# Mean and variance sums by a column of ones, 1/std spread by VectorE transposes, state read in a layer-1 bank

## The chip, the cores and the metric

The kernel runs on one core of one Trainium2 chip. The metric is the time of one execution in microseconds (us); the median of three timed runs is compared. Engines are named TensorE (PE, with its weight loads as PEld), VectorE (DVE), ScalarE (ACT), GpSimd (POOL) and SyncE (SP).

## What is computed

Three stages run one after the other on 8 batches of 512 tokens and 512 channels (8 heads of 64), with 32 state rows per batch and head.

```
scores = x state^T / 8;  a  = softmax(scores);   xread = a state
scores2 = state x^T / 8; a2 = softmax(scores2);  sread = a2 x
x = concat(xread, sread)                           # (8, 544, 512)
mu, var = mean and variance of x over 512 channels
xn = (x - mu) / sqrt(var + 1e-6) * g_ln
x = x + max(xn w_ch1, 0) w_ch2                     # 512 -> 2048 -> 512
gate = sigmoid(5-tap causal convolution of x);  out = ((x w_val) * gate) w_out
```

The weights come as 64-bit floats and are decoded on the chip.

## The kernel before

Channels lie on partitions and tokens in the free dimension, so a sum over channels is a sum over partitions and over KT = 4 column tiles. Matrix products in the feed-forward run as three fp32r matmuls (`mm3`: high and low halves of both operands). Because xread = a state, the first layer is applied to the attention weights: `m_steps` forms m from the state and w_ch1, and a hidden block f is h = m a (two `mm3`, 6 matmuls of 512 columns). ReLU and the split into halves (`hid`) follow on ScalarE and VectorE, and `second(f)` adds the block to four accumulators (four `mm3`, 12 matmuls). `segment` walks f = 0..15 for a batch and lets `second(f)` run one block late. Division by the standard deviation is put off to the end: after the last block, `second` multiplies the accumulators by a row of 1/std, `rstd_row`, and adds x.

The attention of the next batch, the variance and the state read run as `background` generators, one step per block f. TensorE's order is the program's (`manual_schedule`); the other engines' order comes from a scheduler that weighs priorities and expected times. Batches 0 and 1 are special: they run in halves, interleaved with the decoding of the weights, by `first` and `second`, and take mean and variance in `x1_steps`; batches 2 to 7 use `x1_group`, `x1_mean` and `x1_var`. The 256 state-read tokens of all batches form a ninth batch (`sread_block_steps`, key B).

The parts in question:

- `x1_mean` (and lines 358 to 361 for batches 0 and 1): the mean row over all partitions, 6 fp32r matmuls of 512 columns with the column sums of the state, `sbhl`, against the halves of the attention weights.
- `rstd_of`: the squares, summed over the column tiles, are the stationary operand of four fp32 matmuls with one moving column of ones (L293), then VectorE scales (L296) and GpSimd takes the power -1/2 (L297). Each fp32 matmul is recorded as two.
- `rstd_row`: four fp32 matmuls of 128 columns with the identity (L385) turn 1/std into a row on all partitions, and ScalarE copies it (L390). It runs at the end of each half batch.
- `sread`: 32 groups of small matmuls (L276) into a bank of the pool `at`; VectorE transposes it out (L280).

Three PSUM pools exist: four accumulator banks, two `mm` banks for h, two `at` banks for everything else. Scratch tiles of 128x512 share the tag `t2`, six buffers.

Of the kernel before, what the change touches and what calls it, by code (L numbers as in the profile page):

```python
# [21 lines left out]
P = 128  # L22
# [22 lines left out]
def tile_kernel(ctx: ExitStack, tc: tile.TileContext, xT, xk, stT, sn, w1, w2, wval, wout, convw, gln, ident, out):  # L45
# [9 lines left out]
    def sb(shape, dt, tag, bufs=1):  # L55
        cnt[0] += 1
        return main.tile(shape, dt, tag=tag, bufs=BUFS.get(tag, bufs), name=f"{tag}_{cnt[0]}")
# [31 lines left out]
    nhalf = sb([P, KT], F32, "nhalf")  # L89
    ones = sb([P, 1], F32, "ones")  # L90
    nmean = sb([P, 1], F32, "nmean")
# [176 lines left out]
    def sread(b):  # L268
        a2T = a2s.pop(b)
        xn = loads[b][3]  # L270
        sr = at_ps([P, 2, D])
        for u in range(2):
            for c in range(4):
                for p in range(KT):
                    r = slice(32 * p, 32 * p + 32)
                    nc.tensor.matmul(  # L276
                        sr[r, u, :], lhsT=a2T[u][:, c, r], rhs=xn[:, c, 2 * p + u, :], start=(c == 0), stop=(c == 3)
                    )
        srs = t2([P, 4, 32])
        nc.vector.transpose(srs.rearrange("p t n -> p (t n)"), sr.rearrange("p u d -> p (u d)"))  # L280
        for p in range(KT):
            nc.sync.dma_start(
                out=x1d[b, :, p, :].rearrange("(t j) n -> j t n", j=32), in_=srs[32 * p:32 * p + 32]
            )
# [3 lines left out]
    def rstd_of(key, sqs, n):  # L288
        while len(sqs) > 1:
            nc.gpsimd.tensor_tensor(sqs[0], sqs[0], sqs.pop(), op=ALU.add)  # L290
        var = at_ps([P, n // P])
        for c in range(n // P):
            nc.tensor.matmul(var[:, c:c + 1], lhsT=sqs[0][:, c * P:(c + 1) * P], rhs=ones, start=True, stop=True)  # L293
        rstd = small([P, n // P, 1], F32, "rstd")
        rv = rstd.rearrange("p c o -> p (c o)")
        nc.vector.tensor_scalar(rv, var, 1.0 / DM, 1e-6, op0=ALU.mult, op1=ALU.add)  # L296
        nc.gpsimd.tensor_tensor(rv, rv, nhalf[:, :n // P], op=ALU.pow)  # L297
        rstds[key] = rstd
# [16 lines left out]

    def x1_mean(b):
        sbhl, ahl = coef[b][3], ahls[b]
        mus[b] = mu = at_ps([P, S])
        for u in range(2):
            h, l = sbhl[:, 0, u].to_broadcast([P, P]), sbhl[:, 1, u].to_broadcast([P, P])  # L320
            mm3(mu, h, l, ahl[:, u, 0], ahl[:, u, 1], u == 0, u == 1)
# [3 lines left out]
    def x1_var(b):  # L325
# [9 lines left out]
        nc.gpsimd.tensor_tensor(sqs[0], sqs[0], sqs.pop(), op=ALU.add)  # L335
        yield
# [3 lines left out]
        rstd_of(b, sqs, S)  # L340
        yield

    def x1_steps(b):
# [31 lines left out]
        nc.vector.tensor_tensor(sqs[0], sqs[0], sqs.pop(), op=ALU.add)  # L375
        yield
        yield
        rstd_of(b, sqs, S)
        yield

    def rstd_row(key, n):
        rstd = rstds[key]
        rrow = at_ps([P, n])
        for c in range(n // P):
            nc.tensor.matmul(  # L385
                rrow[:, c * P:(c + 1) * P], lhsT=rstd[:, c].to_broadcast([P, P]), rhs=ident_sb,
                start=True, stop=True,
            )
        r = t2([P, n])
        nc.scalar.copy(r, rrow)  # L390
        return r

    def attention_steps(b):
# [13 lines left out]
        softmax1_out(b)  # L407
        yield
# [9 lines left out]
    def sread_block_steps():  # L418
# [3 lines left out]
        yield  # L422
        mu = at_ps([P, NTS])
        for k in range(KT):
            nc.tensor.matmul(mu, lhsT=nmean.to_broadcast([P, P]), rhs=xs[:, k], start=k == 0, stop=k == KT - 1)
# [17 lines left out]
        rstd_of(B, [sq[0][:, 0], sq[0][:, 1]], NTS)  # L443
# [336 lines left out]
    nc.vector.memset(ones, 1.0)  # L780
    nc.vector.memset(nmean, -1.0 / DM)
# [234 lines left out]
```

## Time and profile before

| | us |
|---|---|
| median of three runs | 925.7 |
| the three runs | 924.37, 926.07, 925.7 |
| the profiled execution: span from first to last instruction | 923.6 |
| TensorE busy in it | 905.1 (98%) |
| VectorE, ScalarE, GpSimd busy | 579.0, 374.7, 179.8 |

The profile is of one execution; its own time is known as its span, 923.6 us, which lies 2.1 us under the median of the runs. A matmul's record is longer than the distance between two starts, because matmuls overlap; what one costs is read from the distance of the starts.

### The profile page before, as it was taken

To read this page: it belongs to the slowest core of one execution; us is meant where nothing else is said; L and a number is where in the kernel's file an instruction comes from. 1 tells how busy PE (TensorE), PEld (TensorE's weight loads), DVE (VectorE), ACT (ScalarE), POOL (GpSimd) and SP (SyncE) were. 2 spreads that over 40 slices of the span, in tenths; PEclk is the share of its full clock that TensorE was granted. 3 is DMA by queue.
4 is the path that set the end of the run, shared out by engine and by line. 5 is a ranking of instruction groups with operands and counts; after the bars stand their busy time and mean duration, and the time that the engine had idled before them with its cause. 6 is when DMAs were issued, how large, how long until landed. Compare 5 with 4: busy or idle time off the path is not lost.

```text
span 923.6 us, 12956 instructions
## 1 busy us (share of the span) xinstructions
PE 905.1 (98%) x5151; PEld 687.6 (74%) x5152; DVE 579.0 (63%) x1004; ACT 374.7 (41%) x688; POOL 179.8 (19%) x155
## 2 busy tenths in 40 slices
PE   7989999999999999999999999999999999999998
PEld 2346766777777677777777777777789988888886
DVE  6997987575358571444427246342449799988871
ACT  4755654243234332332324134231326555555532
POOL 0000000012113421411431141141200022433100
PEclk8999999999999999999999999999999999999999
DMA  9932220012103111110101110110111203222122
GB/s 368 358 117 72 72 73 1 41 54 98 49 1 117 49 49 49 49 49 16 70 15 46 49 46 1 27 46 1 46 69 70 82 18 130 91 92 92 46 91 69
DMA packets 26668, 66.45 MB, mean 72 GB/s; under 512 B 10864, under 2 KB 13040, under 8 KB 22512
## 3 DMA queue, kind: packets, MB, share of 16 engines
q1 hardware_dynamic: 25984, 65.24, 19.8%
q8 instruction: 40, 0.66, 0.3%
q10 hardware_dynamic: 624, 0.40, 0.2%
q14 instruction: 20, 0.16, 0.1%
HBM read 47.80 MB, written 17.83 MB: 71 GB/s over the span
## 4 chain that ended last, share of the span: by engine, by line
PE 89%; DVE 5%; ACT 3%; DMA 2%; issue 1%; SPq 0%; ACTq 0%; DVEq 0%
PE acc L77 16%; PE acc L79 16%; PE acc L78 16%; PE mm L77 9%; PE mm L79 8%; PE mm L78 8%; PE at L138 4%; PE at L77 2%; PE at L78 2%; PE at L79 2%; PE mm L914 1%; PE at L276 1%; PE at L385 1%; DMA big<-in_xT 1%; PE at L262 1%
## 5 line engine op out<-in xcount | busy, mean ns | idle before, releaser
L626 DVE SCALAR_TENSOR_TENSOR hid<-mm,hid 128x512 fp32r<-128x512 f32 (+1 forms) x140 | 92.3, 659 | 210.1 <-ACT hid L624 210.0
L77 PE MATMUL acc<-hid,w 128*128 128x512 f32 (+1 forms) x560 | 213.4, 381 | 2.6 <-DVE x L312 1.8
L79 PE MATMUL acc<-hid,w 128*128 128x512 f32 (+1 forms) x560 | 211.5, 378 | 0.0
L78 PE MATMUL acc<-hid,w 128*128 128x512 f32 (+1 forms) x560 | 211.3, 377 | 0.0
L624 ACT ACTIVATE hid<-mm 128x512 fp32r<-128x512 f32 (+2 forms) x144 | 82.5, 573 | 246.4 <-PE mm L79 243.6
L77 PEld LDWEIGHTS acc<-hid,w 128*128 128x128 f32 x560 | 105.4, 188 | 24.8 <-DVE x L312 2.7
L77 PE MATMUL mm<-ahl,m 128*128 128x512 f32 (+1 forms) x312 | 120.9, 388 | 0.0
L79 PEld LDWEIGHTS acc<-hid,w 128*128 128x128 f32 x560 | 105.4, 188 | 20.0
L78 PEld LDWEIGHTS acc<-hid,w 128*128 128x128 f32 x560 | 105.4, 188 | 19.1
L78 PE MATMUL mm<-ahl,m 128*128 128x512 f32 (+1 forms) x312 | 115.3, 369 | 0.0
L79 PE MATMUL mm<-ahl,m 128*128 128x512 f32 (+1 forms) x312 | 115.2, 369 | 0.0
L74 POOL TENSOR_TENSOR m<-mb,m 128x512 fp32r<-128x512 f32 x48 | 65.4, 1379 | 201.6 <-ACT m L73 201.6
L702 DVE SCALAR_TENSOR_TENSOR ahl<-big,cw,ahl 128x508 f32<-128x508 f32 (+3 forms) x128 | 102.8, 852 | 0.2
L77 PEld LDWEIGHTS mm<-ahl,m 128*128 128x128 f32 x312 | 59.0, 189 | 40.5 <-issue 32.5
L73 ACT ACTIVATE m<-mb 128x512 fp32r<-128x512 f32 x62 | 38.8, 629 | 86.6 <-DVE mb L144 86.5
L79 PEld LDWEIGHTS mm<-ahl,m 128*128 128x128 f32 x312 | 59.0, 189 | 10.1
L78 PEld LDWEIGHTS mm<-ahl,m 128*128 128x128 f32 x312 | 59.1, 189 | 8.5 <-DVE m L74 0.5
L144 DVE SCALAR_TENSOR_TENSOR mb<-cs,sbn,at 128x512 f32<-128x512 f32 x62 | 43.5, 743 | 28.3 <-PE at L138 27.5
L688 POOL TENSOR_TENSOR w<-big,w 128x512 fp32r<-128x512 f32 x24 | 38.2, 1621 | 93.7 <-ACT w L686 93.7
L78 PE MATMUL acc<-w,raw 128*128 128x512 f32 (+1 forms) x144 | 54.3, 377 | 0.0
L79 PE MATMUL acc<-w,raw 128*128 128x512 f32 (+1 forms) x144 | 54.3, 377 | 0.0
L77 PE MATMUL acc<-w,raw 128*128 128x512 f32 (+1 forms) x144 | 54.3, 377 | 0.0
(172 smaller groups left out, 1314.5 us busy)
## 6 DMA issues: line engine op xcount, KB each, us to landing
w<-in_w SPq DMA_DIRECT2D x20, 512.0 KB, 7.1
big<-in_xT SPq DMA_DIRECT2D x8, 1024.0 KB, 4.8
big<-in_xk SPq DMA_DIRECT2D x8, 1024.0 KB, 6.5
x2d<-x SPq DMA_DIRECT2D x8, 1024.0 KB, 3.9
big<-x2d SPq DMA_DIRECT2D x8, 1024.0 KB, 4.8
out<-hid SPq DMA_DIRECT2D x16, 512.0 KB, 2.8
raw<-in_w SPq DMA_DIRECT2D x12, 512.0 KB, 6.4
raw<-in_wval SPq DMA_DIRECT2D x4, 512.0 KB, 3.6
```

Source lines behind the costliest of these rows:

```text
L73: nc.scalar.activation(hi, src, AF.Copy)
L74: eng.tensor_tensor(lo, src, hi.bitcast(F32), op=ALU.subtract)
L77: nc.tensor.matmul(acc, lhsT=wh, rhs=xl, start=first, stop=False)
L78: nc.tensor.matmul(acc, lhsT=wl, rhs=xh, start=False, stop=False)
L79: nc.tensor.matmul(acc, lhsT=wh, rhs=xh, start=False, stop=last)
L138: nc.tensor.matmul(mp[u][32 * p:32 * p + 32, :], lhsT=stg[r, p, :], rhs=w1s[4 * q + p][r], start=True, stop=True)
L144: a = nc.vector.scalar_tensor_tensor(mb, cs[:, q], sbn[:, u], mp[u], op0=ALU.mult, op1=ALU.add)
L262: nc.tensor.transpose(tp[:, c, :], a2[u][:, c * P:(c + 1) * P], ident_sb)
L624: marks["act"] = nc.scalar.activation(hid[:, 0], h, AF.Relu)
L626: marks["dve"] = nc.vector.scalar_tensor_tensor(hid[:, 1], h, 0.0, hid[:, 0].bitcast(F32), op0=ALU.max, op1=ALU.subtract)
L688: nc.gpsimd.tensor_tensor(lo, src, hi.bitcast(F32), op=ALU.subtract)
L702: t = nc.vector.scalar_tensor_tensor(g[:, j:], x[:, :n - j], cw_sb[:, k, PAD - j:TAPS - j], g[:, j:], op0=ALU.mult, op1=ALU.add)
```

## The change

- A helper `halves_of` splits a 128 x n tile into fp32r halves: high on ScalarE, low on GpSimd (or on VectorE where it is scaled). `column_total` multiplies both halves by ones on all 128 x 128 weights: two fp32r matmuls of n columns, the total in every partition.
- Mean of batches 2 to 7: `mean_terms` forms state sum times attention weight for both column tiles (one ScalarE and one VectorE instruction) and splits it one batch ahead; `x1_mean` is a `column_total`. Batches 0 and 1 keep theirs.
- Variance of all batches: the summed squares are split and `column_total` gives the row; VectorE transposes it in blocks of 32, scales, GpSimd takes the power of 16 columns in place of 4.
- `rstd_row` is one VectorE transpose of the broadcast 1/std; its matmuls and its ScalarE copy are gone.
- The state read of batches 2 to 7 goes into an `mm` bank.
- The state tokens' mean: two GpSimd additions, a scaled split and a `column_total` in place of four fp32 matmuls (L425), two steps later.

```
--- before.py
+++ after.py
@@ -86,9 +86,8 @@
     ident_sb = sb([P, P], F32, "ident")
     g_sb = sb([P, KT, 1], F32, "g")
     cw_sb = sb([P, KT, TAPS], F32, "cw")
-    nhalf = sb([P, KT], F32, "nhalf")
-    ones = sb([P, 1], F32, "ones")
-    nmean = sb([P, 1], F32, "nmean")
+    nhalf = sb([P, S // 32], F32, "nhalf")
+    ones = sb([P, 1], F32R, "ones")
     part = sb([P, 1], F32, "part")
     cs = sb([P, NQ, S], F32, "cs")
     halos = []
@@ -268,7 +267,7 @@
     def sread(b):
         a2T = a2s.pop(b)
         xn = loads[b][3]
-        sr = at_ps([P, 2, D])
+        sr = ps(ps_mm, "mm", [P, 2, D]) if b > 1 else at_ps([P, 2, D])
         for u in range(2):
             for c in range(4):
                 for p in range(KT):
@@ -285,16 +284,28 @@
 
     x1s, rstds = {}, {}
 
-    def rstd_of(key, sqs, n):
-        while len(sqs) > 1:
-            nc.gpsimd.tensor_tensor(sqs[0], sqs[0], sqs.pop(), op=ALU.add)
-        var = at_ps([P, n // P])
-        for c in range(n // P):
-            nc.tensor.matmul(var[:, c:c + 1], lhsT=sqs[0][:, c * P:(c + 1) * P], rhs=ones, start=True, stop=True)
-        rstd = small([P, n // P, 1], F32, "rstd")
+    def halves_of(x, n, scale=1.0):
+        hi, lo = (sb([P, n], F32R, "t2") for _ in range(2))
+        nc.scalar.activation(hi, x, AF.Copy, scale=scale)
+        if scale == 1.0:
+            nc.gpsimd.tensor_tensor(lo, x, hi.bitcast(F32), op=ALU.subtract)
+        else:
+            nc.vector.scalar_tensor_tensor(lo, x, scale, hi.bitcast(F32), op0=ALU.mult, op1=ALU.subtract)
+        return hi, lo
+
+    def column_total(out, hl):
+        for i in range(2):
+            nc.tensor.matmul(out, lhsT=ones.to_broadcast([P, P]), rhs=hl[i], start=i == 0, stop=i == 1)
+
+    def rstd_of(key, hl, n):
+        var = at_ps([P, n])
+        column_total(var, hl)
+        turned = t2([P, n // 32, 32])
+        nc.vector.transpose(turned.rearrange("p g n -> p (g n)"), var)
+        rstd = small([P, n // 32, 1], F32, "rstd")
+        nc.vector.tensor_scalar(rstd, turned[:, :, :1], 1.0 / DM, 1e-6, op0=ALU.mult, op1=ALU.add)
         rv = rstd.rearrange("p c o -> p (c o)")
-        nc.vector.tensor_scalar(rv, var, 1.0 / DM, 1e-6, op0=ALU.mult, op1=ALU.add)
-        nc.gpsimd.tensor_tensor(rv, rv, nhalf[:, :n // P], op=ALU.pow)
+        nc.gpsimd.tensor_tensor(rv, rv, nhalf[:, :n // 32], op=ALU.pow)
         rstds[key] = rstd
 
     def x1_group(b):
@@ -313,12 +324,18 @@
             else:
                 nc.scalar.copy(x1[:, k], xp[k])
 
+    def mean_terms(b):
+        sbn, aT = coef[b][2], aTs[b]
+        t = t2([P, S])
+        nc.scalar.activation(t, aT[:, 0], AF.Copy, scale=sbn[:, 0])
+        nc.vector.scalar_tensor_tensor(t, aT[:, 1], sbn[:, 1], t, op0=ALU.mult, op1=ALU.add)
+        terms[b] = halves_of(t, S)
+
+    terms = {}
+
     def x1_mean(b):
-        sbhl, ahl = coef[b][3], ahls[b]
         mus[b] = mu = at_ps([P, S])
-        for u in range(2):
-            h, l = sbhl[:, 0, u].to_broadcast([P, P]), sbhl[:, 1, u].to_broadcast([P, P])
-            mm3(mu, h, l, ahl[:, u, 0], ahl[:, u, 1], u == 0, u == 1)
+        column_total(mu, terms.pop(b))
 
     mus = {}
 
@@ -333,11 +350,12 @@
             else:
                 sqs.append(xc)
         nc.gpsimd.tensor_tensor(sqs[0], sqs[0], sqs.pop(), op=ALU.add)
-        yield
-        yield
-        yield
-        yield
-        rstd_of(b, sqs, S)
+        hl = halves_of(sqs[0], S)
+        yield
+        yield
+        yield
+        yield
+        rstd_of(b, hl, S)
         yield
 
     def x1_steps(b):
@@ -373,22 +391,16 @@
                 sqs.append(xc)
         x1s[b] = x1
         nc.vector.tensor_tensor(sqs[0], sqs[0], sqs.pop(), op=ALU.add)
-        yield
-        yield
-        rstd_of(b, sqs, S)
+        hl = halves_of(sqs[0], S)
+        yield
+        yield
+        rstd_of(b, hl, S)
         yield
 
     def rstd_row(key, n):
-        rstd = rstds[key]
-        rrow = at_ps([P, n])
-        for c in range(n // P):
-            nc.tensor.matmul(
-                rrow[:, c * P:(c + 1) * P], lhsT=rstd[:, c].to_broadcast([P, P]), rhs=ident_sb,
-                start=True, stop=True,
-            )
-        r = t2([P, n])
-        nc.scalar.copy(r, rrow)
-        return r
+        r = t2([P, n // 32, 32])
+        nc.vector.transpose(r, rstds[key].to_broadcast([P, n // 32, 32]))
+        return r.rearrange("p g n -> p (g n)")
 
     def attention_steps(b):
         state_coefs(b)
@@ -405,6 +417,7 @@
         softmax2_turn(b)
         yield
         softmax1_out(b)
+        mean_terms(b)
         yield
         sread(b)
         yield
@@ -420,9 +433,14 @@
         for k in range(KT):
             nc.sync.dma_start(out=xs[:, k].rearrange("p (b n) -> p b n", n=NS), in_=x1d[:, :, k, :].rearrange("b p n -> p b n"))
         yield
+        t = t2([P, 2, NTS])
+        nc.gpsimd.tensor_tensor(t, xs[:, :2], xs[:, 2:], op=ALU.add)
+        nc.gpsimd.tensor_tensor(t[:, 0], t[:, 0], t[:, 1], op=ALU.add)
+        hl = halves_of(t[:, 0], NTS, -1.0 / DM)
+        yield
+        yield
         mu = at_ps([P, NTS])
-        for k in range(KT):
-            nc.tensor.matmul(mu, lhsT=nmean.to_broadcast([P, P]), rhs=xs[:, k], start=k == 0, stop=k == KT - 1)
+        column_total(mu, hl)
         xc = sb([P, KT, NTS], F32, "big")
         xn = sb([P, 2, KT, NTS], F32R, "ahl")
         for k in range(KT):
@@ -440,7 +458,11 @@
         for i in range(2):
             nc.scalar.activation(sq[i], xc[:, 2 * i:2 * i + 2], AF.Square)
         nc.gpsimd.tensor_tensor(sq[0], sq[0], sq[1], op=ALU.add)
-        rstd_of(B, [sq[0][:, 0], sq[0][:, 1]], NTS)
+        nc.gpsimd.tensor_tensor(sq[0][:, 0], sq[0][:, 0], sq[0][:, 1], op=ALU.add)
+        hl = halves_of(sq[0][:, 0], NTS)
+        yield
+        yield
+        rstd_of(B, hl, NTS)
         yield
 
     def load_raw(tag, src):
@@ -777,8 +799,7 @@
             yield
 
     nc.vector.memset(nhalf, -0.5)
-    nc.vector.memset(ones, 1.0)
-    nc.vector.memset(nmean, -1.0 / DM)
+    nc.vector.memset(ones.bitcast(F32), 1.0)
     nc.vector.memset(part, 1.0 / 32)
     order = [("2", 0), ("2", 1), ("1", 4), ("2", 2), ("1", 5), ("1", 6), ("2", 3), ("1", 7)]
     order += [("2", f) for f in range(4, 8)]
```

What moves on the engines is seen at three places. In these rows a name stands before its buffer and tile numbers, `t` is a scratch tile, `at` and `mm` are banks.

TensorE, first hidden blocks of batch 4, behind the block f = 1; before (the last three rows follow once more):

```order
L78 MATMUL mm_3253<-ahl_3015,m_3091 128x512
L79 MATMUL mm_3253<-ahl_3015,m_3091 128x512
L77 MATMUL at_3260<-ahl_3015,sbhl_2821 128x512
L78 MATMUL at_3260<-ahl_3015,sbhl_2821 128x512
L79 MATMUL at_3260<-ahl_3015,sbhl_2821 128x512
```

and now:

```order
L78 MATMUL mm_3250<-ahl_3010,m_3093 128x512
L79 MATMUL mm_3250<-ahl_3010,m_3093 128x512
L298 MATMUL at_3257<-t_545_3018,ones_82 128x512
L298 MATMUL at_3257<-t_546_3019,ones_82 128x512
L77 MATMUL acc_586_3263<-hid_3183,w_0_89_434 128x512
L78 MATMUL acc_586_3263<-hid_3183,w_0_89_434 128x512
```

Six matmuls of the mean have become two; the accumulation of the block before follows at once.

VectorE, batch 1's attention inside batch 0, from the transposes of the scores (L193, L192 now) to the first negated maximum (L244, L243 now), which ScalarE's exponential waits for; before:

```order
L193 STREAM_TRANSPOSE t_118_557<-at_547 128x512
L193 STREAM_TRANSPOSE t_119_559<-at_548 128x512
L243 TENSOR_REDUCE nmax_563<-at_547 128x1
L243 TENSOR_REDUCE nmax_563<-at_548 128x1
L74 TENSOR_TENSOR w_6_126_579<-c_578,w_6_126_579 128x512
L201 TENSOR_REDUCE mxden_571<-t_118_557 128x16
L201 TENSOR_REDUCE mxden_571<-t_119_559 128x16
L244 TENSOR_SCALAR nmax_563<-nmax_563 128x1
L626 SCALAR_TENSOR_TENSOR hid_595<-mm_588,hid_595 128x512
```

and now (L648 is the hidden split L626, L493 the decode step L471):

```order
L74 TENSOR_TENSOR w_6_127_581<-c_580,w_6_127_581 128x512
L192 STREAM_TRANSPOSE t_119_559<-at_549 128x512
L192 STREAM_TRANSPOSE t_120_561<-at_550 128x512
L242 TENSOR_REDUCE nmax_565<-at_549 128x1
L242 TENSOR_REDUCE nmax_565<-at_550 128x1
L200 TENSOR_REDUCE mxden_573<-t_119_559 128x16
L200 TENSOR_REDUCE mxden_573<-t_120_561 128x16
L648 SCALAR_TENSOR_TENSOR hid_597<-mm_590,hid_597 128x512
L493 TENSOR_SCALAR c_626<-c_626 128x512
L243 TENSOR_SCALAR nmax_565<-nmax_565 128x1
```

The low half of a decoded weight (L74) went from behind the maxima to ahead of the transposes, and a hidden split and a decode step now stand ahead of the negated maximum.

ScalarE, the same batch, from the softmax normalization (L254, L253 now) to the second of the two copies (L264, L263 now) that free the `at` banks of TensorE's transposes; before:

```order
L254 ACTIVATE t_120_561<-t_120_561,r_180_893 128x512
L254 ACTIVATE t_121_562<-t_121_562,r_180_893 128x512
L264 COPY t_143_688<-at_683 128x512
L624 ACTIVATE hid_751<-mm_697 128x512
L463 ACTIVATE w_4_154_770<-raw_138 128x512
L465 ACTIVATE raw_138<-raw_138 128x512
L264 COPY t_145_695<-at_690 128x512
L223 ACTIVATE ahl_678<-aT_675 128x512 x2
```

and now (L222 is the split L223 of batch 1's attention weights, L646 the ReLU L624, L485 and L487 the decode steps L463 and L465):

```order
L253 ACTIVATE t_121_563<-t_121_563,r_181_890 128x512
L253 ACTIVATE t_122_564<-t_122_564,r_181_890 128x512
L73 ACTIVATE m_646<-mb_647 128x512
L646 ACTIVATE hid_662<-mm_655 128x512
L73 ACTIVATE m_646<-mb_651 128x512
L222 ACTIVATE ahl_680<-aT_677 128x512
L263 COPY t_144_690<-at_685 128x512
L646 ACTIVATE hid_753<-mm_699 128x512
L485 ACTIVATE w_4_156_772<-raw_136 128x512
L487 ACTIVATE raw_136<-raw_136 128x512
L222 ACTIVATE ahl_680<-aT_677 128x512
L263 COPY t_146_697<-at_692 128x512
```

The two splits L222, which need VectorE's transposes of the attention weights, went from behind both copies to ahead of each.

## Rows read from the trace of the kernel before

**Rows 1.** The page's first line.

```profile
span 923.6 us, 12956 instructions
```

**Rows 2.** Windows: us, then busy time (count) of five engines, PEclk, DMA share, GB/s.

```profile
70.00:72.00 2.00, 2.00 (x17) 0.62 (x3) 2.00 (x5) 1.21 (x2) 0.00 (x0) 0.50 0.00 0
92.00:110.00 18.00, 17.43 (x94) 12.76 (x93) 18.00 (x36) 10.29 (x19) 0.00 (x0) 1.00 0.30 92
306.00:640.00 334.00, 334.00 (x2020) 254.88 (x2019) 147.20 (x259) 102.01 (x186) 93.17 (x80) 1.00 0.11 35
```

**Rows 3.** Groups by line: the two kinds of fp32 matmuls.

```profile
L385 PE MATMUL at<-ident,rstd 128*128 128x128 f32 x84 | 11.1, 274 | 0.0
...
L293 PE MATMUL at<-ones,t 128*128 128x1 f32 x68 | 8.2, 241 | 0.0
```

**Rows 4.** Timeline of TensorE, end of batch 3: start, us, instruction.

```profile
449.96 0.39 PE L77 MATMUL mm<-ahl,m 128*128 128x512 f32 x1
...
451.32 1.05 PE L385 MATMUL at<-ident,rstd 128*128 128x128 f32 x8
...
452.44 0.39 PE L78 MATMUL acc<-hid,w 128*128 128x512 f32 x1
```

**Rows 5.** Timeline of TensorE, variance of batch 4.

```profile
480.32 0.95 PE L293 MATMUL at<-ones,t 128*128 128x1 f32 x8
...
481.45 0.39 PE L78 MATMUL mm<-ahl,m 128*128 128x512 f32 x1
```

**Rows 6.** Timeline of TensorE, mean of the state tokens.

```profile
646.02 1.89 PE L425 MATMUL at<-big,nmean 128*128 128x256 f32 x8
...
647.98 0.39 PE L78 MATMUL mm<-ahl,m 128*128 128x512 f32 x1
```

**Rows 7.** Timeline of TensorE: behind a state read, and elsewhere.

```profile
436.06 1.59 PE L138 MATMUL at<-w,stg 64*32 64x512 f32 x16
437.59 0.50 PE L77 MATMUL mm<-ahl,m 128*128 128x512 f32 x1
...
455.08 1.09 PE L138 MATMUL at<-w,stg 64*32 64x512 f32 x16
456.10 0.68 PE L307 MATMUL acc<-aT,sn_raw 32*64 32x512 f32 x8
```

**Rows 8.** Waits of TensorE: us in total, times, longest.

```profile
PE acc L77 <- DVE x L312: 1.8, 2, 1.4
```

**Rows 9.** Timeline of all engines in batch 0; in brackets idle time before.

```profile
67.65 0.15 DVE L244 TENSOR_SCALAR nmax<-nmax 128x1 f32<-128x1 f32 x1
67.71 0.69 DVE L626 SCALAR_TENSOR_TENSOR hid<-mm,hid 128x512 fp32r<-128x512 f32 x1
...
68.36 0.42 DVE L471 TENSOR_SCALAR c<-c 128x512 f32<-128x512 f32 x1
...
68.72 2.62 PE L138 MATMUL at<-w,stg 64*32 64x512 f32 x16 [1.99 <-ACT t L245]
...
78.33 0.95 PE L293 MATMUL at<-ones,t 128*128 128x1 f32 x8
78.53 0.60 ACT L624 ACTIVATE hid<-mm 128x512 fp32r<-128x512 f32 x1 [1.13 <-PE mm L79]
...
79.16 0.69 DVE L626 SCALAR_TENSOR_TENSOR hid<-mm,hid 128x512 fp32r<-128x512 f32 x1 [1.00 <-ACT hid L624]
...
79.77 0.70 DVE L218 STREAM_TRANSPOSE aT<-t 128x512 f32<-128x512 f32 x1
80.13 0.57 ACT L264 COPY t<-at 128x512 f32<-128x512 f32 x1
...
80.76 1.10 PE L276 MATMUL at<-big,t 128*32 128x64 f32 x64 [1.47 <-ACT t L264]
```

**Rows 10.** Timeline of GpSimd and VectorE in batch 3.

```profile
419.71 3.00 POOL L74 TENSOR_TENSOR m<-mb,m 128x512 fp32r<-128x512 f32 x2 [1.14 <-ACT m L73]
...
420.16 1.39 DVE L224 TENSOR_TENSOR ahl<-aT,ahl 128x512 fp32r<-128x512 f32 x1
...
422.64 0.68 DVE L224 TENSOR_TENSOR ahl<-aT,ahl 128x512 fp32r<-128x512 f32 x1
```

## The prediction

> **What bounds the kernel now.** I read the page first: the span is 923.6 us [rows 1], and TensorE is busy for 905.1 us of it. An average hides stages, so I read the windows by stretch next. From 306 to 640 us, where batches 3 to 7 run, TensorE is busy for all 334 us at a granted clock of 1.00 (2.4 GHz), while VectorE has work for 147.2, ScalarE for 102.0 and GpSimd for 93.2 us [rows 2]. There a TensorE instruction taken away is time taken away, and other engines' work is hidden unless TensorE comes to wait for it. Before about 130 us it is otherwise: from 92 to 110 us VectorE is busy for 18.00 of 18 us and TensorE has gaps [rows 2]. The chain of batches 0 and 1 runs through VectorE and ScalarE too, and an instruction put in the wrong place there can cost.
>
> What a matmul costs is read from the distance of starts, since its record is longer. In [rows 4] six fp32r matmuls of 512 columns start from 449.96 to 451.32, where the next kind starts: 1.36 / 6 = 0.227 us each. All savings below are counted in this unit.
>
> **What the change takes from TensorE.** (A) *1/std row.* The eight records of L385 start at 451.32 and the next kind at 452.44; one ordinary matmul is the last distance, so the block costs 1.12 - 0.23 = 0.89 us [rows 4]. There are 84 records [rows 3]: ten blocks of eight, and four for the state tokens. 10 x 0.89 + 0.45 = 9.4 us. Nothing replaces them on TensorE.
>
> (B) *Variance.* L293 starts at 480.32, the next kind at 481.45: 1.13 - 0.23 = 0.90 us [rows 5]. Two fp32r matmuls of 512 columns, 0.45, take its place, so 0.45 is saved; 68 records [rows 3] are eight batches and a half one, 8 x 0.45 + 0.2 = 3.8 us.
>
> (C) *Mean* of batches 2 to 7: six matmuls become two, 4 x 0.227 = 0.91, times six: 5.4 us.
>
> (D) *State tokens' mean.* 646.02 to 647.98 less one distance is 1.73 us [rows 6]; two matmuls of 256 columns cost about one of 512, 0.23. Saved: 1.5 us.
>
> (E) *State read.* The 16 matmuls of L138 that stand behind a state read take 436.06 to 437.59 = 1.53 us, others 455.08 to 456.10 = 1.02 [rows 7]. The difference, 0.51, I read as the wait for VectorE's transpose of the read to free the `at` bank. In an `mm` bank, which is wanted again only later, it goes: 5 x 0.51 = 2.6 us for batches 3 to 7.
>
> (F) *Batch 2's wait.* TensorE waits 1.8 us in all for the x1 copies of L312 [rows 8]. The first copy now comes ahead of a decode pair. Bounds 0 and 1.8; I take 0.5, since other VectorE work remains ahead.
>
> Sum: 9.4 + 3.8 + 5.4 + 1.5 + 2.6 + 0.5 = 23.2 us.
>
> **What it adds, and what covers that.** Each batch from 2 on gains on VectorE a scaled addition and two transposes, about 0.70 us each by the transpose L218 [rows 9], on ScalarE three activations of about 0.6 [rows 9] (one copy of the row goes), on GpSimd two subtractions of about 1.5, by the pair of L74 in 3.00 [rows 10]. A hidden block is 18 x 0.227 = 4.1 us of TensorE, and VectorE is 44% busy there [rows 2]; the variance's halves have four blocks, 16 us, before they are used. I cost them at nothing; without that cover a subtraction would cost TensorE its 1.5 us. The GpSimd power now takes 16 columns instead of 4, and is needed at least 6 us later. The transpose of a broadcast (stride 0) is an operation that the trace does not show: from below 0.70 [rows 9] as an ordinary transpose; from above I know only that the source repeats one element 32 times. I take 0.70, since it writes the same tile. It is read about four blocks' products later, and one that took longer would first use up VectorE's idle half. The scratch tiles are tight at a batch's end: high, low, row and four products want seven of six buffers, so the fourth product waits for GpSimd's first addition, 0.70 + 1.50 = 2.2 us after the first product's start, while VectorE's four steps take 4 x 0.70 = 2.8 at the price of the scaled addition and the transpose: covered by 0.6 us.
>
> **What it moves in batches 0 and 1.** The orders quoted with the change show three places; their prices are the trace's.
>
> (a) TensorE waits 1.99 us at 68.72 for the exponential [rows 9], which waits for the negated maximum (67.65). Ahead of that now stand a hidden split (0.69) and a decode step (0.42) [rows 9], and the low half of a decoded weight stands ahead of the transposes, which I put at 0.3, for part of it fills idle time: +1.4 us, the wait becomes 3.4.
>
> (b) The two copies L264 free the banks that the variance's sum and the state read want. The first, early today, now stands behind a split that needs VectorE's transpose of the attention weights. That transpose starts at 79.77 after a split (79.16) that waited 1.00 us for ScalarE's ReLU [rows 9]. Without that wait and with the split of L626 behind it (0.6 by the distance of the starts), but 1.4 late by (a), it ends at 80.47 - 1.00 - 0.6 + 1.4 = 80.3. A split of 0.6 and the copy of 0.57 follow: 81.5. TensorE comes there at 78.33 + 1.4 = 79.75 and waits 1.75. The second copy (80.13 today, with two decode steps in the 1.00 us behind the ReLU) comes behind ReLU 0.6, decode steps 1.0 and split 0.6: 81.5 + 2.2 + 0.57 = 84.3. The state read, at 80.76 today, 0.06 behind this copy, starts at about 84.4: 3.6 later, of which 1.4 is (a). That is +2.2 us, as a second wait of about 2.4 where today's is 1.47.
>
> (c) In batch 1 the same two copies stand behind a ReLU, four decode steps and the new split, some 6 x 0.55 = 3.3 us later (ScalarE's steps are 0.50 to 0.60 [rows 9]), where TensorE hardly waits today. Bounds 0 and 3.3; I take 1.4, because the copies have some lead.
>
> (d) *Clock.* After the wait of 1.99 us the granted clock is 0.50 (1.2 GHz) from 70 to 72 us, and L138 takes 2.62 instead of 1.09 us [rows 2, 7, 9]. A new wait of 1.75 us at 80 us may do the same to the 64 matmuls behind it. Bounds 0 and 1.5; I take 1.2, between them and nearer to the drop that was seen, 2.62 - 1.09 = 1.5.
>
> Losses: 1.4 + 2.2 + 1.4 + 1.2 = 6.2 us. Net 23.2 - 6.2 = 17.0. The profiled execution would take 923.6 - 17.0 = 906.6; it lies 2.1 under the median of the runs, so the time is **908.7 us**.
>
> **A rule that speaks against it.** In the trace VectorE's subtraction L224 took 1.39 us beside GpSimd's L74, and 0.68 by itself [rows 10]: 0.71 of delay. The Trainium skill, "SBUF — State Buffer", section "SBUF: two separate sides", says why: VectorE with two SBUF inputs and GpSimd share one port pair, which whoever is first holds for its whole instruction. This case's trace agrees, with the 1.39 against 0.68. The change adds 15 GpSimd subtractions (6 means, 8 variances, one small), 15 x 0.71 = 10.7 us of delay at most. By the rows, the delay falls on VectorE, which is 44% busy, and the sum stays; as a rival it has its line below.
>
> **Rivals.**
> 1. *The early waits do not come* (0.2). The copies come with slack or TensorE's later waits shrink by as much, as when a stall only moves. Then 923.6 - 23.2 + 2.1 = 902.5. For it: before 130 us VectorE is the fuller engine [rows 2] and sheds no work here, so a wait earlier can be one less later. Against it: VectorE gets more to do there, too.
> 2. *The early losses double* (0.18): each moved copy costs its upper bound and later steps of the decode follow: 12.5 us, so 915.0.
> 3. *Port* (0.04): all 10.7 us of GpSimd's delays reach TensorE: 919.4. Against it: an idle half of VectorE's time.
> 4. *Slower: the transpose of the broadcast* (0.03). It stands right ahead of the products that free the accumulators; at x us over 0.70, ten full rows and a half one hold TensorE. Of the 0.6 us cover four batch ends keep some, so 4x + 6(x - 2.3) is the loss, and it reaches the gain of 17 us plus the 1.9 that can be told at x = 3.3, or 4.0 us for one. At 5 us each (x = 4.3) it is 17.2 + 12 = 29 us: 938. For it: no such source in the trace. Against it: the tile written is that of L218.
>
> **How the numbers follow.** The forecast has 0.55, with its own range 904.5 to 912.5 from (c), (d) and (F) at their ends: 908.7 - 1.4 - 1.2 - 1.3 and 908.7 + 1.9 + 0.3 + 0.5, rounded outwards for (a) and (b). To hold eight in ten, with rival 1 below and half of rival 2 above, the range is 901.5 to 914.5. A measurement of this kernel can tell about 0.2%, 1.9 us; cases 1 to 3 and the forecast all lie further under 925.7. Faster 0.96, same 0.01 (a transpose near 4 us), slower 0.03.
>
> **What the profile would show.** Right: at a batch's end L77 starts follow at 0.227 us up to the next accumulation, with no matmul for the row; two matmuls for each mean and variance; L138 behind a state read at 1.02; a wait near 3.4 us at 70 us for the exponential, and two of about 1.75 and 2.4 at 80 to 84 us for ScalarE's copies; less than 1.8 us for the x1 copies. Wrong: TensorE waiting for VectorE at batch ends from 306 us on (scratch tiles or the broadcast transpose); new waits between 84 and 130 us larger than (c); matmuls with column-of-ones weights that do not keep the 0.227 pitch.

## The result and the profile after

The changed kernel takes 911.1 us (910.09 to 911.17, four runs) against 925.6 for the kernel before: a ratio of 0.9846, 95% interval 0.9832 to 0.9860. It is faster by 14.5 us, or 1.5%. The forecast was 908.7 with a range of 901.5 to 914.5. The profiled execution's span is 908.0 where 906.6 was forecast; the rest of the distance, 1.0 us, is that this span lies 3.1 us under the median of the runs instead of 2.1, because the fastest of the four executions was profiled.

The page's first line and the windows of the changed kernel (columns as in [rows 2]):

```profile
span 908.0 us, 12667 instructions
```

```profile
70.00:72.00 2.00, 2.00 (x16) 0.22 (x14) 2.00 (x7) 1.66 (x5) 0.00 (x0) 0.65 0.00 0
92.00:110.00 18.00, 17.92 (x95) 13.10 (x96) 17.97 (x36) 11.12 (x21) 0.00 (x0) 1.00 0.27 92
306.00:640.00 334.00, 333.87 (x1997) 253.56 (x1998) 157.43 (x276) 109.28 (x198) 116.15 (x91) 1.00 0.11 35
```

TensorE is still busy for the whole stretch of 306 to 640 us, so the 10 us that VectorE gained there, the 7 of ScalarE and the 23 of GpSimd are hidden, as costed. Groups by line, VectorE and then GpSimd, show the new instructions:

```profile
L402 DVE STREAM_TRANSPOSE t<-rstd 128x512 f32<-128x512 f32 (+1 forms) x11 | 7.2, 657 | 1.5 <-POOL rstd L308 1.5
L304 DVE STREAM_TRANSPOSE t<-at 128x512 f32<-128x512 f32 (+1 forms) x9 | 6.1, 681 | 12.6 <-PE at L298 12.6
```

```profile
L308 POOL TENSOR_TENSOR rstd<-rstd,nhalf 128x16 f32<-128x16 f32 (+1 forms) x9 | 25.2, 2801 | 40.9 <-DVE rstd L306 40.9
L291 POOL TENSOR_TENSOR t<-t,t 128x512 fp32r<-128x512 f32 (+1 forms) x15 | 19.6, 1310 | 128.8 <-ACT t L289 128.8
```

These means mix in the one half-size instruction of the state tokens. With full tiles alone the transpose of the broadcast row (L402) takes 0.68 us and that of the variance (L304) 0.71, so a repeated source costs no more than a full one: its rival falls. On TensorE's timeline of batches 4 and 5 each removed piece is seen where [rows 4, 5 and 7] showed it (counted by the ends of the batches, the row in [rows 4] is that of batch 4 and the variance in [rows 5] that of batch 5):

```profile
430.93 1.10 PE L275 MATMUL mm<-big,t 128*32 128x64 f32 x64
431.96 1.09 PE L137 MATMUL at<-w,stg 64*32 64x512 f32 x16
432.98 0.50 PE L77 MATMUL mm<-ahl,m 128*128 128x512 f32 x1
...
446.49 0.40 PE L79 MATMUL mm<-ahl,m 128*128 128x512 f32 x1
446.72 0.40 PE L77 MATMUL acc<-hid,w 128*128 128x512 f32 x1
446.96 0.40 PE L78 MATMUL acc<-hid,w 128*128 128x512 f32 x1
...
474.04 0.63 PE L298 MATMUL at<-t,ones 128*128 128x512 f32 x2
474.51 0.39 PE L77 MATMUL mm<-ahl,m 128*128 128x512 f32 x1
474.74 0.40 PE L78 MATMUL mm<-ahl,m 128*128 128x512 f32 x1
```

The small matmuls behind the state read take 1.02 us (431.96 to 432.98), the accumulation follows the last hidden block with no row between, and the variance is two matmuls in 0.47. With the second matmul behind a place as the mark, as in the prediction, the row's place took 1.12 us before [rows 4] and takes 0.24 now (446.72 to 446.96): 0.88 saved. The variance took 1.13 [rows 5] and takes 0.70 (474.04 to 474.74): 0.43 saved. Further behind, where the pitch is the same again in both kernels, the gain is 0.87 for a row and 0.46 for a variance. The waits of TensorE, where they changed (us in total, times, longest):

```profile
PE at L137 <- ACT t L244: 3.1, 1, 3.1
...
PE at L275 <- ACT t L263: 1.3, 1, 1.3
PE acc L77 <- DVE x L323: 1.3, 1, 1.3
...
PE at L275 <- DVE t L304: 1.1, 1, 1.1
...
PE at L298 <- ACT t L263: 0.3, 1, 0.3
```

How far the changed kernel is ahead is read by following one instruction through both traces (start before, start after, and what lies between two places):

| the same TensorE instruction | before | after | ahead | in this stretch |
|---|---|---|---|---|
| accumulation ahead of the exponential's wait | 63.85 | 63.83 | 0.02 | |
| last accumulation of batch 0 | 174.41 | 174.70 | -0.29 | three rows and two variances save 3.5, so 3.8 lost |
| last accumulation of batch 2 | 293.09 | 290.21 | 2.88 | 3.2; rows, variance, mean and state read save 3.6, so 0.4 lost |
| fourth hidden block behind the end of batch 2 | 314.30 | 313.29 | 1.01 | mean and the rest of a row save 1.0, so 2.9 lost |
| accumulation in the state tokens' part | 649.14 | 635.38 | 13.76 | 12.8 |
| first matmul of the last stage | 733.50 | 717.85 | 15.65 | 1.9 |

Two stretches lose much: batches 0 and 1, as forecast in kind, and the end of batch 2, which was not. In the kernel before, that place looks like this (timelines of VectorE and TensorE):

```profile
293.78 0.68 DVE L478 CUSTOM_DVE_ANT_0 c<-raw,c 128x1024 uint16<-128x1024 uint16 x1
294.38 2.48 DVE L653 TENSOR_TENSOR t<-acc,t 128x512 f32<-128x512 f32 x4
...
297.06 1.11 PE L307 MATMUL acc<-aT,sn_raw 32*64 32x512 f32 x16
298.11 0.50 PE L77 MATMUL mm<-ahl,m 128*128 128x512 f32 x1
```

In the changed kernel it looks like this (timeline of all engines, with TensorE's other matmuls left out; in brackets the idle time before):

```profile
291.11 0.69 DVE L675 TENSOR_TENSOR t<-acc,t 128x512 f32<-128x512 f32 x1 [2.19 <-PE acc L79]
291.72 0.42 DVE L495 TENSOR_SCALAR c<-c 128x512 uint32<-128x512 uint32 x1
291.88 1.41 POOL L678 TENSOR_TENSOR x<-t,x 128x512 f32<-128x512 f32 x1 [10.39 <-DVE t L675]
292.05 1.86 DVE L496 TENSOR_SCALAR raw<-raw 128x512 uint16<-128x512 uint16 x1
293.70 0.73 DVE L675 TENSOR_TENSOR t<-acc,t 128x512 f32<-128x512 f32 x1
294.12 2.63 PE L318 MATMUL acc<-aT,sn_raw 32*64 32x512 f32 x12
294.33 0.69 DVE L648 SCALAR_TENSOR_TENSOR hid<-mm,hid 128x512 fp32r<-128x512 f32 x1
294.93 0.69 DVE L675 TENSOR_TENSOR t<-acc,t 128x512 f32<-128x512 f32 x1
295.53 0.81 DVE L500 CUSTOM_DVE_ANT_0 c<-raw,c 128x1024 uint16<-128x1024 uint16 x1
296.26 0.68 DVE L675 TENSOR_TENSOR t<-acc,t 128x512 f32<-128x512 f32 x1
296.99 1.07 PE L318 MATMUL acc<-aT,sn_raw 32*64 32x512 f32 x4 [0.24 <-DVE t L675]
```

The four products L675 free the four accumulators, into which L318 forms x1 of the next batch. Because the row is there early, VectorE takes the first product as soon as its accumulator is done, and between this product and the others stand three steps of the decoding of w_val (L495, L496, L500) and a hidden split. The products reach from 291.11 to 296.94. The sixteen L318 take from 294.12 to 297.99, 3.9 us; before, the same block (L307) took 1.05, 297.06 to 298.11. The wait profile names 0.24 of this: most of it is hidden inside a group of twelve records. Smaller losses of the same kind stand at other batch ends, where a hidden split now stands between the first product and the other three: 0.5 at the end of batch 1 (the block at 217 us takes 2.34 instead of 1.86), and 0.1 at each end of batches 3 to 6 (1.14 instead of 1.04). In the run with the old row, below, those four take 1.04 again.

### The profile page after: what moved, and what is told of

Same layout as the page of the kernel before. It is cut to its first block, busy times and chain, and to the rows that moved or that the text cites. A ratio compares the mean times of both kernels' runs of the same rounds, so it can differ in the third digit from the quotient of the medians.

```text
span 908.0 us, 12667 instructions
## 1 busy us (share of the span) xinstructions
PE 887.1 (98%) x4987; PEld 668.5 (74%) x4988; DVE 595.7 (66%) x1030; ACT 381.9 (42%) x699; POOL 216.3 (24%) x172
## 4 chain that ended last, share of the span: by engine, by line
PE 81%; DVE 12%; DMA 3%; ACT 1%; issue 1%; SPq 0%; DVEq 0%; ACTq 0%
PE acc L77 15%; PE acc L79 15%; PE acc L78 15%; PE mm L77 9%; PE mm L78 8%; PE mm L79 8%; PE at L137 3%; PE at L77 2%; PE at L79 2%; PE at L78 2%; DVE w L496 1%; DVE w L500 1%; DMA x1d<-t 1%; DVE hid L648 1%; DVE raw L496 1%
## 5 line engine op out<-in xcount | busy, mean ns | idle before, releaser
L648 DVE SCALAR_TENSOR_TENSOR hid<-mm,hid 128x512 fp32r<-128x512 f32 (+1 forms) x140 | 92.0, 657 | 141.4 <-ACT hid L646 141.2
L646 ACT ACTIVATE hid<-mm 128x512 fp32r<-128x512 f32 (+2 forms) x144 | 82.4, 572 | 216.6 <-PE mm L79 212.9
L74 POOL TENSOR_TENSOR m<-mb,m 128x512 fp32r<-128x512 f32 x48 | 65.4, 1377 | 142.3 <-ACT m L73 142.3
L143 DVE SCALAR_TENSOR_TENSOR mb<-cs,sbn,at 128x512 f32<-128x512 f32 x62 | 43.5, 743 | 21.9 <-PE at L137 20.9
```

The costliest lines, as they stand in the source:

```text
L74: eng.tensor_tensor(lo, src, hi.bitcast(F32), op=ALU.subtract)
L143: a = nc.vector.scalar_tensor_tensor(mb, cs[:, q], sbn[:, u], mp[u], op0=ALU.mult, op1=ALU.add)
L646: marks["act"] = nc.scalar.activation(hid[:, 0], h, AF.Relu)
L648: marks["dve"] = nc.vector.scalar_tensor_tensor(hid[:, 1], h, 0.0, hid[:, 0].bitcast(F32), op0=ALU.max, op1=ALU.subtract)
```

## The experiments

All are edits of the changed kernel, timed beside the kernel before. The expectations put the losses of batches 0 and 1 at 4.3 us; over the whole stretch, with 0.8 that went the other way at 109 us and with the savings as the traces give them, they are the 3.8 of the table. They also take a row at 0.80 and a variance at 0.35, which is the distance to the very next matmul; the gain that stays is 0.87 and 0.46. So where they say 11.4 us for all rows and variances, the traces give 13.1, and 4.4 instead of 3.9 for batches 0 and 1.

**Old variance and row everywhere**:

```
-        hl = halves_of(sqs[0], S)
...
-        rstd_of(b, hl, S)
+        rstd_of(b, sqs, S)
...
-        column_total(var, hl)
+        for c in range(n // P):
+            nc.tensor.matmul(var[:, c:c + 1], lhsT=sqs[0][:, c * P:(c + 1) * P], rhs=ones.bitcast(F32), start=True, stop=True)
...
-        nc.vector.transpose(r, rstds[key].to_broadcast([P, n // 32, 32]))
+                rrow[:, c * P:(c + 1) * P], lhsT=rstd[:, c].to_broadcast([P, P]), rhs=ident_sb,
...
+        nc.scalar.copy(r, rrow)
```

> Variance by four small fp32 matmuls and the 1/std row by TensorE, as before, for all batches; mean, state read and state tokens' mean stay changed. In the changed kernel's trace ten rows save 0.80 us each and the half one 0.36 (8.4), nine variances about 0.35 each (3.0), together 11.4 us; against that stand 4.3 us of new waits in batches 0 and 1 and 2.8 us at the end of batch 2, where the products that free the accumulators are spread between decode steps. Theory: these 7.1 us of losses come from the new variance and row alone, so undoing both costs 11.4 - 7.1 = 4.3 us: 915.4 us, with the early waits at their old 2.0 and 1.5 us and the four products at the end of batch 2 in one piece. Rival 1: the losses come from the other parts or from the rest of the new order, so undoing costs the whole 11.4: 922.5 us. Rival 2: only the early losses belong to it: 918.2 us.

Measured: 916.3 us (914.51 to 917.73), ratio to the kernel before 0.9895, 0.9879 to 0.9912. That is 5.2 over the changed kernel. With the prices of the traces the theory comes to 13.1 - 7.1 = 6.0 us, the two rivals to 13.1 and 8.8, so they fall. In batches 3 to 6 of its trace the changed kernel gets 0.87 us further ahead at each row and 0.46 at each variance. The exponential's wait is 1.99 again (1.1 won back), the wait ahead of the state read of batch 1 goes (1.3), and the products of batch 2 stand three in one piece (VectorE's timeline), which wins back 2.3:

```profile
292.76 0.68 DVE L502 CUSTOM_DVE_ANT_0 c<-raw,c 128x1024 uint16<-128x1024 uint16 x1
293.36 1.88 DVE L677 TENSOR_TENSOR t<-acc,t 128x512 f32<-128x512 f32 x3
295.16 0.80 DVE L74 TENSOR_TENSOR raw<-c,raw 128x512 fp32r<-128x512 f32 x1
295.88 0.68 DVE L677 TENSOR_TENSOR t<-acc,t 128x512 f32<-128x512 f32 x1
```

So both losses belong to the new variance and row. With the old mean or the old state read, below, the exponential's wait stays at 3.1, and with the old state read 2.9 us are lost at the end of batch 2 as before: these two have no part in them.

**Old variance and row in batches 0 and 1 alone:**

```
     def rstd_of(key, hl, n):
+        if key < 2:
+            var = at_ps([P, n // P])
+            for c in range(n // P):
+                nc.tensor.matmul(var[:, c:c + 1], lhsT=hl[:, c * P:(c + 1) * P], rhs=ones.bitcast(F32), start=True, stop=True)
...
     def rstd_row(key, n):
+        if key < 2:
+            rrow = at_ps([P, n])
...
+            nc.scalar.copy(r, rrow)
+            return r
```

> Variance and 1/std row as before in batches 0 and 1 only; batches 2 to 7 and the state tokens as in the changed kernel. The orders of VectorE and ScalarE in batches 0 and 1 are then those of the kernel before. Theory: this costs 4 x 0.80 + 2 x 0.35 = 3.9 us of TensorE and gives back 4.3 us of waits: 910.7 us, even with the changed kernel; the loss at the end of batch 2 (2.8 us) stays. Rival: the waits are not the new order's, so they stay: 915.0 us. Second rival: a wait taken away early turns into another one behind it in the decode, then 912 to 914.

Measured: 910.6 us (909.45 to 913.06), ratio 0.9843, 0.9825 to 0.9861: even with the changed kernel, as the theory has it. The waits at 69 and 80 us are 1.97 and 1.47 again. The two profiled executions differ in the clock as well (last section): behind the wait at 69 us this one keeps 1.00, and it falls to 0.51 at the end of batch 2, where the changed kernel's stays at 1.00. From 65 us to the end of batch 0 this kernel gains 1.7 us on the changed one, which is no more than the first of these differences gives. So up to there the new variance and row bring nothing: what TensorE saves it waits.

**The decode of w_val divided over batches 2 and 3:**

```
+        for k in ks:
...
-        if b == 2:
-            yield from prep_weights(wval, wv, ["raw"] * KT)
+        if b in (2, 3):
+            yield from prep_weights(wval, wv, ["raw"] * KT, range(2 * b - 4, 2 * b - 2))
```

> Two of the four tiles of w_val are decoded in the last blocks of batch 2 and two in those of batch 3, instead of all four in batch 2; nothing else differs from the changed kernel. Theory: at the end of batch 2 the early row lets VectorE take the four products one by one between decode steps, which GpSimd's additions slow; with half the decode the products come closer together and most of the loss of 2.8 us and of the 1.6 us of waits behind it goes: 3 us less, 908 us. Rival 1: the products are spread whatever the decode does: 911.1 us. Rival 2: the end of batch 3 now loses what that of batch 2 gains: 911 us, with new waits near 371 us.

Measured: 905.0 us (904.69 to 905.42), ratio 0.9776, 0.9761 to 0.9790. The timeline at the end of batch 2:

```profile
291.18 0.69 DVE L675 TENSOR_TENSOR t<-acc,t 128x512 f32<-128x512 f32 x1 [2.53 <-PE acc L79]
291.78 0.68 DVE L648 SCALAR_TENSOR_TENSOR hid<-mm,hid 128x512 fp32r<-128x512 f32 x1
291.95 5.03 POOL L678 TENSOR_TENSOR x<-t,x 128x512 f32<-128x512 f32 x4 [10.39 <-DVE t L675]
292.38 1.87 DVE L675 TENSOR_TENSOR t<-acc,t 128x512 f32<-128x512 f32 x3
...
294.18 1.20 PE L318 MATMUL acc<-aT,sn_raw 32*64 32x512 f32 x16
```

The row is as early as in the changed kernel, but the products end at 294.25, and L318 has no stop. Against the changed kernel 2.7 us are won up to the next hidden block, 1.6 more where the x1 copies L323 were waited for, and 0.8 in the two accumulations behind: 5.1 of span. The gain is larger than expected because the copies' wait, which the kernel before has too [rows 8], goes as well. No new wait comes at the end of batch 3. The early row without decode steps behind it costs only the 0.1 of the other batch ends; the early row among decode steps costs the 2.9. Dividing the decode is a change of its own: no run has it in the kernel before, so how much of the 5.1 that kernel would gain too is not shown; its wait for the copies, 1.8, could go there.

**Both together:**

> Both of the above: old variance and row in batches 0 and 1, and the decode of w_val divided over batches 2 and 3. Theory: the two effects are in different places and add: 910.7 + 908 - 911.1 = 907.6 us. Rival: they don't add, because the decode of the weights reaches from batch 1 into batch 2 and a delay in the one changes the other: over 909.

Measured: 906.3 us (903.89 to 907.29), ratio 0.9786, 0.9767 to 0.9805. The sum of the two by their measured times would be 910.6 + 905.0 - 911.1 = 904.5, at the edge of what these runs allow; it isn't better than the divided decode alone. In the profiled executions the two are level at the end of batch 0; the old row then puts this one 0.35 behind at the end of batch 1, and 0.58 goes into a wait for a hidden split at 684 us.

**Divided decode, and no split of the squares in batches 0 and 1:**

```
-        hl = halves_of(sqs[0], S)
         yield
         yield
-        rstd_of(b, hl, S)
+        rstd_of(b, sqs[0], S)
...
-        column_total(var, hl)
+        if key < 2:
+            nc.tensor.matmul(var, lhsT=ones.bitcast(F32).to_broadcast([P, P]), rhs=hl, start=True, stop=True)
+        else:
+            column_total(var, hl)
```

> As the kernel with the divided decode of w_val (905.0 us), and in batches 0 and 1 the squares are not split into halves: their sum over the partitions is one fp32 matmul of 512 columns against the ones, with the broadcast row and its transpose as changed. The orders of ScalarE and VectorE in batches 0 and 1 are then nearly those of the kernel before, as far as the copies that free the banks and the negated maximum. Theory: the 4.3 us of early waits come from the two splits (a ScalarE and a GpSimd instruction and two scratch tiles each), not from the row: they go, and an fp32 matmul of 512 columns costs four passes, 0.91, for 0.45, twice: 905.0 - 4.3 + 0.9 = 901.6 us. Rival: the early waits belong to the new transposes and the 16-column power, which stay: 905.9 us.

Measured: 902.8 us (901.59 to 902.98), ratio 0.9756, 0.9742 to 0.9769. This version beats both kernels: 22 us under the kernel before. Its largest waits behind the first 10 us:

```profile
PE at L137 <- ACT t L244: 2.0, 1, 2.0
PE at L275 <- ACT t L263: 1.4, 1, 1.4
```

They are those of the kernel before [rows 9], though the row is still VectorE's transpose. Against the divided decode alone 2.2 us are won by the medians, with the two fp32 matmuls paid for; by the ratios, each to the kernel before beside it, it is 1.9, with an uncertainty of about 1.8. Of the 3.3 us that the profiled execution gained by 115 us about 1.6 is the clock, which fell behind the exponential's wait in the one and not in the other (see the last section). What is left, 1.7, is less than the 3.4 that the theory has, also because a wait of 0.76 for VectorE at 107 us is back, which the kernel before has too (0.57). But the exponential's wait is the old one and the one at 115 us is gone. So the exponential's 1.1 us and the state read's 1.4 at 115 us come from splitting the squares there, with the order that follows, not from the row. Whether the two scratch tiles or the two instructions of a split turn the order was not separated.

**Old mean in batches 2 to 7:**

```
-        column_total(mu, terms.pop(b))
...
+            mm3(mu, h, l, ahl[:, u, 0], ahl[:, u, 1], u == 0, u == 1)
...
-        mean_terms(b)
```

> Mean of batches 2 to 7 by six matmuls as before, without the terms formed ahead; all else as in the changed kernel. Theory: TensorE pays 0.92 us in each of six batches, 5.5; in the one behind batch 2, TensorE waits for copies anyway (1.31 us), so between 4.6 and 5.5: 915.7 to 916.6 us. Rival: the instructions for the terms, with GpSimd's subtraction, cost something through VectorE or the port, and undoing them gives that back: under 914.

Measured: 914.9 us (914.08 to 915.45), ratio 0.9887, 0.9873 to 0.9901. In the trace the mean costs 0.91 net in each of batches 4 to 7. In batch 2 it costs 0.4 net, because the block L318 ahead of it is 0.6 shorter, and behind the end of batch 2 nothing: there this kernel is 1.93 us behind the changed one ahead of the mean and 1.81 two blocks later. In this execution the wait for the copies is gone there and the granted clock is 0.51 from 299.5 to 303 us. That makes 4.0 us, and the medians give 3.8, both under the expectation. The spans differ by 5.2; the other 1.2 are lost near 92 us, where VectorE waits 1.27 for a DMA that still reads a scratch tile, with the same order of instructions as the changed kernel. No part shows a gain from the instructions that went.

**State read back in an `at` bank:**

```
-        sr = ps(ps_mm, "mm", [P, 2, D]) if b > 1 else at_ps([P, 2, D])
+        sr = at_ps([P, 2, D])
```

> State read of batches 2 to 7 back in an at bank; all else as in the changed kernel. Theory: TensorE waits 0.5 us again behind each of five or six reads: 2.6 to 3.1 us more, 913.7 to 914.2. Rival: the wait was only taken over from a later one, and 911.1 stays.

Measured: 913.6 us (912.72 to 919.03, one of six executions over 914), ratio 0.9882, 0.9861 to 0.9902; that is 2.4 over the changed kernel. In the trace 0.50 to 0.51 us come back at five places.

**Additions of batch 2 on VectorE:**

```
-                        eng = nc.vector if b < 2 or b >= B - 1 else nc.gpsimd
+                        eng = nc.vector if b < 3 or b >= B - 1 else nc.gpsimd
```

> The additions of x to the products of batch 2 run on VectorE instead of GpSimd; the spread order of the products at the end of batch 2 stays. Rival theory for the loss there, the shared port: the decode step took 1.86 us beside GpSimd's addition and 0.74 by itself, so without the additions on GpSimd it takes 0.74, the products come 1 to 2 us sooner, and the time is about 909.5. My theory: the order is what costs, VectorE now has the additions between the products as well (4 x 0.69), and the time is 911 to 912.5, though the decode step takes its 0.74 us again.

Measured: 910.4 us (909.22 to 911.88), ratio 0.9840, 0.9825 to 0.9855, which doesn't tell 909.5 from 911. VectorE's timeline tells more:

```profile
292.85 0.69 DVE L675 TENSOR_TENSOR t<-acc,t 128x512 f32<-128x512 f32 x1 [2.19 <-PE acc L79]
293.46 0.42 DVE L495 TENSOR_SCALAR c<-c 128x512 uint32<-128x512 uint32 x1
293.79 0.75 DVE L496 TENSOR_SCALAR raw<-raw 128x512 uint16<-128x512 uint16 x1
294.32 0.72 DVE L675 TENSOR_TENSOR t<-acc,t 128x512 f32<-128x512 f32 x1
...
296.16 0.68 DVE L675 TENSOR_TENSOR t<-acc,t 128x512 f32<-128x512 f32 x1
...
297.96 0.68 DVE L675 TENSOR_TENSOR t<-acc,t 128x512 f32<-128x512 f32 x1
```

L496 takes 0.75 instead of 1.86 when GpSimd adds nothing beside it. From the first product to the fourth it is still 5.1 us, since two additions now stand between them. From the last accumulation of batch 2 to the fourth hidden block behind it TensorE takes 21.9 us here, and 23.1 in the changed kernel. Both put GpSimd's share at about 1.1 of the 2.9; the order is the larger part.

## Why the prediction was right

The time lies inside the range, and the mechanism, TensorE's time taken away and a part given back in batches 0 and 1, is the measured one. The savings (A) to (E) came as forecast. That the total comes so close is partly luck: the early losses were put too high, and losses at the batch ends were left out.

- **(A) row:** 0.87 to 0.89 where it can be followed, against 0.89, ten times, and 0.45: 9.2 against 9.4. The first matmul behind a row starts 0.81 behind the row's start, but the distance to the second is 0.32 instead of 0.23, and that does not come back.
- **(B) variance:** 0.46 in batches 3 to 7, 0.21 for the state tokens: 3.9 if the first batches are like the others, against 3.8.
- **(C) mean** 6 x 0.9 = 5.4, **(D)** 1.5 (old block 1.75 of TensorE, the new one 0.26), **(E)** 5 x 0.51: as forecast.
- **(F) is the step that failed.** I forecast 0.5 us gained on the wait for the x1 copies at the end of batch 2. The copies' wait fell from 1.8 to 1.3, but 2.9 us were lost there in all, because the four products ahead of the copies were spread over 5.8 us. The prediction looked at these products for scratch tiles only, and put the early row at no cost. The old row, which came last, had kept VectorE's products together. The runs show it from two sides: the old row brings the products together again (2.3 us), and so does taking decode steps away (5.1 us with the copies' wait). The same step leaves out the 0.5 at the end of batch 1 and the 0.1 at each of four later ends.
- **(a)** 1.1 against 1.4: the exponential's wait is 3.11. The reading of the order was right.
- **(b)** was mis-sized. The variance waits 0.31 for its bank, not 1.75, because VectorE's transpose of the attention weights ended at 78.93 and not at 80.3: the delay of (a) did not reach it. The hidden block ahead of the variance is 1.3 us later than before, the accumulation behind the state read 1.5: with the variance's saving about 0.6 is lost between them, not 2.2. The state read waits first for VectorE's transpose of the variance (L304, 1.12), a wait that the change adds and that the prediction does not list; its second half then waits 0.3 for ScalarE's second copy, inside the group.
- **(c)** a wait of 1.34 for ScalarE's copy at 115 us, against 1.4, and 0.44 behind it for a hidden split. On the other side 0.6 for VectorE's L367 at 109 us went.
- **(d)** no second fall of the clock: in 80 to 84 us it is 1.00. The early losses net 3.8 us up to 174 instead of 6.2.
- The gains come to 22.5 and the losses to 3.8 + 0.4 + 2.9 + 0.4 = 7.5; a wait of 0.73 for a hidden split in the state tokens' part also went. 22.5 - 7.5 + 0.7 = 15.7, and the spans differ by 15.6.

Of the rivals, the early waits did come, and cost about six tenths of the forecast. The port cost nothing in 306 to 640 us, where TensorE has 0.13 us without work. It did act at the end of batch 2, though not on the subtractions that I had counted: L496, 1.86 beside GpSimd's addition and 0.75 without. The Trainium skill, "SBUF — State Buffer", section "SBUF: two separate sides", has whichever starts first hold the shared port pair for its whole instruction, against a VectorE instruction with two SBUF inputs or in a two-port mode. The times agree: L496 starts 0.17 behind the addition of 1.41 us and ends 0.62 behind its end. But L496 has one input, and no run shows whether it ran in such a mode.

## What to carry to other kernels

Taking work off the engine that bounds pays at the distance of its starts, and here that could be worked out to within a few hundredths of the sum; measure it up to the second instruction behind, since the distance to it changes too. When a result is made earlier, look at what its lateness kept together: instructions that were issued in one piece may now be issued one by one with other work between them, and the engine behind them waits for the last. In a stage where every engine is full, a cheaper matmul that needs two more small instructions elsewhere can be worth less than the plain one: in batches 0 and 1 one fp32 matmul was no worse than the two split ones, and probably better.

## What was not expected of the hardware

GpSimd's power took 1.39 us for four columns in batch 1 and 2.91 for sixteen (means 1.17 and 2.95 for these shapes); it was hidden here. After the wait for the exponential at 69 us the granted clock fell to 0.50 (1.2 GHz) in some executions and not in others, with the same order of instructions there: behind the wait of 2.0 us it is 0.50 from 70 to 72 us in the kernel before [rows 2], and stays at 1.00 (2.4 GHz) in the kernel with the old variance in batches 0 and 1, whose window is this:

```profile
70.00:72.00 2.00, 2.00 (x21) 1.13 (x7) 2.00 (x6) 1.23 (x2) 0.00 (x0) 1.00 0.00 0
```

Of the profiles with a wait of 2.0 us three of five show the fall, of those with 3.1 us all five. It is worth about 1.5 us (from an accumulation near 65 us to the next behind the wait, the executions with the fall take 9.3 to 9.6 us, those without 8.0 to 8.1), so in comparisons of single executions a difference of that size at this place proves nothing on its own. The same is seen at the end of batch 2. Of the five executions in which the sixteen matmuls L318 are drawn out there over 3.85 us or more, two fall to 0.5 behind it, the one with the old variance in batches 0 and 1 (first line) and the one with the old mean; the changed kernel (second line) does not:

```profile
296.00:303.00 7.00, 6.96 (x16) 4.30 (x17) 6.49 (x10) 4.34 (x9) 5.09 (x5) 0.51 0.63 234
...
296.00:303.00 7.00, 5.93 (x25) 3.31 (x21) 6.46 (x10) 4.05 (x7) 6.00 (x5) 1.00 0.64 235
```

What decides it these runs do not show.
